# Window attention, forward and backward, on one core: P and dS of five quads turned on TensorE, and the first loads in another order

## The chip, the cores and the metric

The kernel runs on one core of a Trainium2 chip. The core has TensorE (PE in the profile: matrix products; PEld is its loading of weights), VectorE (DVE), ScalarE (ACT), GpSimd (POOL) and SyncE (SP). SyncE, ScalarE and GpSimd issue transfers (DMA) here; each issues its own in the order of its instructions, and an instruction that waits holds up what stands behind it on the same engine. The metric is the device time of one execution in microseconds (us). Before the change it is 1906.21, the median of three runs (1904.59 to 1907.18).

## The reference

An image `x` of 256 x 256 pixels with 384 channels is cut into 1024 windows of 8 x 8 pixels. In each window the 64 pixels attend to each other with one head, and the result goes through `wo`. The kernel returns this output and the gradients with respect to `x`, `wqkv` and `wo` for a given `grad_out`, all in bfloat16.

```python
qkv = xw @ wqkv                                   # xw: [1024, 64, 384]
q, k, v = qkv[..., :C], qkv[..., C:2 * C], qkv[..., 2 * C:]
p = softmax(einsum('bqc,bkc->bqk', q, k) * C ** -0.5)
o = einsum('bqk,bkc->bqc', p, v) @ wo
# and the vector-Jacobian product of this with grad_out: dx, dwqkv, dwo
```

## The kernel before

**Folded weights.** The kernel never forms q, k and v. It folds the weights into two 384 x 384 matrices: A from Q and K with the scale, B from V and `wo`. For that it needs the three column blocks of `wqkv` and `wo` in SBUF, turns each block on TensorE (`turn_blocks`, line 99) and multiplies them (`weight_product`, line 109). B turned is `BT_sb`, A turned is `AT_sb`.

**Quads.** The work goes in 128 quads. A quad has eight windows, held as four tiles (t = 0 to 3) of 128 partitions, each tile being two windows of 64 pixels; `LO` and `HI` are the two halves. For a quad the kernel loads `xq` (x) and `dq` (the gradient), needs both turned (`xT`, `dT`, channels on the partitions), and makes from them `yz` (the projections of x by A and of the gradient by B). From `yz` and `xT` come the scores and the raw gradient of P together (`sd`), from these the softmax P and its gradient dS (`ps`, both in one tile), and from P, dS and their transposes (`PS`) the outputs: `o` (output rows), `d` (gradient rows of x), and `Uq`, `Wq`, which go into the weight gradients.

**Three quads in flight.** `step(c, b, a, ahead)` (line 373) is one step of the loop. It does the scores, softmax and `uq`/`vq` products of quad b = i, the projections of quad a = i + 1, the attention of quad c = i - 1, and issues the loads of quad `ahead` = i + 4. From step 4 on it also does weight-gradient products of finished groups of three quads (`gf_rows`, `gf_halves`; tiles `pg`, `ph`). TensorE's order within a step is: scores `sd`, eight products `pj` for `uq` and `vq`, projection of the gradient (kind 0), projection of x (kind 1), `gf_rows`, then the attention's tiles `pw`, `pu`, `po`, `pd`, with `gf_halves` between them. The order of every engine is the order in which the program is written (`manual_schedule`). The products go to eight PSUM banks that are used in turn (`ring`), so a product waits until the tile eight places before it has been copied out.

**What waits for what around the change.**

- `soft` (line 203) is the softmax in six parts on VectorE, with one exponential on ScalarE. Part 0 begins with the maximum of the scores, `mx` (line 208); the text uses its start as the mark of a step. Part 5 makes dS.
- The transposes of P and dS are made in two ways. For most quads `turn` (line 258) does it on VectorE, with one transpose of 32 x 32 blocks and four moves (lines 267 and 271). For the quads with `crossed` (0 to 3 and the last, line 420) it is a DMA: `stack` (line 242) copies P into the tile `cr` on ScalarE, part 5 of `soft` writes dS into it with two more subtractions on VectorE (line 239), and SyncE issues a DMA transpose `PS<-cr` (line 264). `cr` has one buffer.
- SyncE's queue takes, in each iteration: `load_turn` of quad i + 2 (DMA transposes `dT<-dq` and `xT<-xq`, line 151), `to_tokens` of quad i (the DMA transpose `tok<-zy`, line 188), `PS<-cr` in the five crossed quads, and the four loads of `xq` of quad i + 4 (line 144). Quad 3 is loaded at the start of iteration 0 and quad 4 in step 0.
- `gather` (line 180) copies `yz` to `zy` on VectorE in two parts, the second in the middle of the attention; `zy` has two buffers, so it waits for the `tok` transfer of two quads before. `tok` is used by the attention one step later.
- GpSimd's queue takes the four `dq` loads of a quad (line 142) and the outputs `o` and `d` (lines 316 to 325).

**The start.** `fetch_weights` (line 75) loads V's columns of `wqkv` and `wo`, each split over SyncE and ScalarE. `load_first` (line 128) loads the gradient of quad 0 over both in turn, then Q's columns on SyncE and K's on ScalarE (`fetch_rest`), then x of quad 0 on SyncE; a copy on GpSimd holds that engine until the last gradient tile has landed. TensorE does seven products on zeros (`warm_up`), turns V, makes `BT_sb`, turns the gradient of quad 0, turns Q, projects, turns K and x of quad 0, makes A, turns the gradient of quad 1 and projects again. `wo` itself is turned after step 1 (line 499). **The end** runs `gf_final` and `weight_gradients`.

Of the kernel before, what the change touches and what calls it, by code (L numbers as in the profile page):

```python
# [9 lines left out]
ALU = mybir.AluOpType  # L10
# [4 lines left out]
P = 128  # L15
# [8 lines left out]
def kernel(  # L24
# [50 lines left out]
    def fetch_weights():  # L75
        wo_in = wo.rearrange("(m p) n -> p m n", p=P)
        nc.sync.dma_start(out=w_sb[:, 0:2, columns(2)], in_=w_in[:, 0:2, columns(2)])
        nc.scalar.dma_start(out=w_sb[:, 2, columns(2)], in_=w_in[:, 2, columns(2)])
        nc.scalar.dma_start(out=wo_sb[:, 0:2, :], in_=wo_in[:, 0:2, :])
        nc.sync.dma_start(out=wo_sb[:, 2, :], in_=wo_in[:, 2, :])  # L80

    def fetch_rest():
        nc.sync.dma_start(out=w_sb[:, :, columns(0)], in_=w_in[:, :, columns(0)])
        nc.scalar.dma_start(out=w_sb[:, :, columns(1)], in_=w_in[:, :, columns(1)])
# [14 lines left out]
    def turn_blocks(dst, src, first=0):  # L99
        for k in range(CK):  # L100
# [3 lines left out]
            copy_out(k, dst[:, k, :], pt[:])  # L104

    def weight_product(dst, left, right, sc):
        for mr in range(CK):
# [4 lines left out]
            if sc is not None:  # L112
                nc.scalar.activation(out=dst[:, mr, :], in_=pc[:], func=ACT.Copy, scale=sc)
            else:
                copy_out(mr, dst[:, mr, :], pc[:])
# [12 lines left out]
    def load_first(st):  # L128
        st["xq"] = xq = grp.tile([P, QUAD, C], BF16, tag="xq", name="xq", bufs=2 * GQ + 5)
        st["dq"] = dq = qp.tile([P, QUAD, C], BF16, tag="dq", name="dq", bufs=6)  # L130
        for t in range(QUAD):
            (nc.sync, nc.scalar)[t % 2].dma_start(out=dq[:, t, :], in_=windows(grad_out, st, 2 * t))
        fetch_rest()
        for t in range(QUAD):
            nc.sync.dma_start(out=xq[:, t, :], in_=windows(x, st, 2 * t))
        nc.gpsimd.tensor_copy(out=spare[:, 0:1], in_=dq[:, QUAD - 1, 0:1])

    def load(st):
# [4 lines left out]
        for t in range(QUAD):  # L143
            nc.sync.dma_start(out=xq[:, t, :], in_=windows(x, st, 2 * t))
# [58 lines left out]
    def soft(st, step):  # L203
# [29 lines left out]
        else:  # L233
            pd = sm.tile([P, QUAD, WT], F32, tag="pd")
            nc.vector.tensor_tensor(out=pd[:], in0=st["Pb"], in1=over_k(st["D"][:]), op=ALU.mult)
            if st["crossed"]:
                cr = st["cr"]
                for w, h, o in ((0, LO, HI), (1, HI, LO)):
                    nc.vector.tensor_tensor(out=cr[o, :, w, :], in0=st["pr"][h, :, :], in1=pd[h, :, :], op=ALU.subtract)
            nc.vector.tensor_tensor(out=st["dS"], in0=st["pr"][:], in1=pd[:], op=ALU.subtract)  # L240

    def stack(st):
        if st["crossed"]:
            st["cr"] = cr = qp.tile([P, QUAD, 2, WT], BF16, tag="cr", name="cr", bufs=1)
            for w, h in ((0, LO), (1, HI)):
                nc.scalar.copy(out=cr[h, :, w, :], in_=st["Pb"][h, :, :])
# [11 lines left out]
    def turn(st):  # L258
        ps = st["ps"]
        st["PS"] = dst = qp.tile([P, 2, QUAD, WT], BF16, tag="PS", name="PS")  # L260
        if st["crossed"]:
# [111 lines left out]
    def step(c, b, a, ahead):  # L373
# [31 lines left out]
        for rows in range(1 if a is not None else 2):  # L405
            if fill:
                gf_rows(*fill.pop(0))
# [133 lines left out]
```

## Time and profile before

| What | Before |
|---|---|
| median of three runs | 1906.21 us (1904.59 to 1907.18) |
| profiled execution, its own time | 1906.89 us |
| its span | 1905.1 us |
| TensorE busy | 1892.1 us (99%) |
| VectorE busy | 1667.7 us (88%) |
| ScalarE busy | 1526.8 us (80%) |
| share of TensorE in the chain that ended last | 96% |
| `sd`: mean of one, 128x64 | 193 ns |
| `tok<-zy`, issue to landing, median | 7.8 us |
| `PS<-cr`, issue to landing, least / median / most | 2.5 / 4.8 / 7.1 us |

The page of a profile gives the busy time of each engine, the chain of work that ended last (followed back from the last instruction, at each step to what released it), and groups of equal instructions. Other views answer questions on a stretch of time: the timeline (start, duration, engine, line, operation, and in brackets how long the engine was idle before and what released it), the waits (who waited for what: total us, times, longest), the chain in order of time (start, duration, what), and windows (busy time of each engine, the clock granted to TensorE as PEclk, the busy share of the DMA engines and GB/s in each stretch). "SPq" and "ACTq" are the sequencers of SyncE and ScalarE; the duration of a DMA there is that of its issue, not of the transfer. TensorE's matmuls are pipelined, so their durations overlap; the distance between starts tells more.

### The profile page before, as it was taken

To read this page: it belongs to the slowest core of one execution; us is meant where nothing else is said; L and a number is where in the kernel's file an instruction comes from. 1 tells how busy PE (TensorE), PEld (TensorE's weight loads), DVE (VectorE), ACT (ScalarE), POOL (GpSimd) and SP (SyncE) were. 2 spreads that over 40 slices of the span, in tenths; PEclk is the share of its full clock that TensorE was granted. 3 is DMA by queue.
4 is the path that set the end of the run, shared out by engine and by line. 5 is a ranking of instruction groups with operands and counts; after the bars stand their busy time and mean duration, and the time that the engine had idled before them with its cause. 6 is when DMAs were issued, how large, how long until landed. Compare 5 with 4: busy or idle time off the path is not lost.

```text
span 1905.1 us, 57100 instructions
## 1 busy us (share of the span) xinstructions
PE 1892.1 (99%) x22333; PEld 1127.1 (59%) x22333; DVE 1667.7 (88%) x3613; ACT 1526.8 (80%) x3355; POOL 861.8 (45%) x1572
## 2 busy tenths in 40 slices
PE   9999999999999999999999999999999999999999
PEld 5565655655665566556555655665566556556655
DVE  5888888888888888888888888888888888888887
ACT  7877887888788888878887888788788878887884
POOL 4444444444454445444444544444445445444432
PEclk9999999999999999999999999999999999999999
DMA  9999999999999999999999999999999999999994
GB/s 208 218 226 204 219 222 230 217 217 216 223 220 214 222 216 219 218 210 228 216 217 206 228 217 223 217 219 214 220 221 219 217 212 222 223 216 221 195 202 104
DMA packets 949647, 408.34 MB, mean 214 GB/s; under 512 B 831232, under 2 KB 924864, under 8 KB 949376
## 3 DMA queue, kind: packets, MB, share of 16 engines
q1 hardware_dynamic: 873056, 253.08, 77.6%
q0 software_dynamic: 75072, 150.72, 31.4%
q8 instruction: 175, 2.87, 0.6%
q10 hardware_dynamic: 1248, 0.89, 0.2%
q14 instruction: 96, 0.79, 0.1%
HBM read 101.84 MB, written 101.84 MB: 107 GB/s over the span
## 4 chain that ended last, share of the span: by engine, by line
PE 96%; DMA 2%; ACT 1%; DVE 1%; issue 0%; DVEq 0%; ACTq 0%
PE pj L162 51%; PE pg L162 13%; PE ph L351 13%; PE sd L162 5%; PE pw L296 5%; PE pu L296 4%; PE po L296 4%; DMA tok<-zy 1%; PE pd L296 1%; DMA w_sb<-in_wqkv_dram 0%; DMA PS<-cr 0%; PE pe L429 0%; ACT yz L176 0%; ACT yz L178 0%; PE pt L103 0%
## 5 line engine op out<-in xcount | busy, mean ns | idle before, releaser
L316 POOL DMA_DIRECT2D out_dram<-o x512 | 274.5, 536 | 897.3 <-ACT o L300 885.3
L307 ACT CAST Wq<-pw 128x384 bf16<-128x384 f32 x506 | 244.0, 482 | 280.4 <-PE pw L296 280.3
L162 PEld LDWEIGHTS <-xT 128*128 128x128 bf16 x3072 | 291.7, 98 | 182.5 <-issue 0.5
L162 PE MATMUL pj<-B_sb,xT 128*128 128x384 bf16 x1536 | 333.4, 326 | 0.1
L162 PE MATMUL pj<-AT_sb,xT 128*128 128x384 bf16 x1536 | 333.3, 326 | 0.0
L142 POOL DMA_DIRECT2D dq<-in_grad_out_dram x508 | 268.8, 537 | 96.1 <-DMA out_dram<-d 38.3
L310 DVE CAST Uq<-pu 128x384 bf16<-128x384 f32 x512 | 283.1, 553 | 13.2 <-PE pu L296 1.1
L318 POOL DMA_DIRECT2D out_dram<-d x480 | 279.3, 582 | 15.4 <-ACT uq L256 6.8
L162 PE MATMUL pj<-dT,BT_sb 128*128 128x512 bf16 x1152 | 269.5, 379 | 0.0
L162 PE MATMUL pj<-xT,A_sb 128*128 128x512 bf16 x1152 | 269.5, 379 | 0.0
L296 PE MATMUL pd<-tok,ps 64*64 64x384 bf16 x2048 | 257.3, 327 | 1.9 <-DMA tok<-zy 1.5
L176 ACT CAST yz<-pj 128x512 bf16<-128x512 f32 x384 | 224.0, 587 | 36.7 <-PE pj L162 28.4
L300 ACT CAST o<-po 128x384 bf16<-128x384 f32 x512 | 249.8, 488 | 1.5 <-PE po L296 1.1
L256 ACT CAST vq<-pj 128x384 bf16<-128x384 f32 x512 | 247.0, 482 | 3.2
L256 ACT CAST uq<-pj 128x384 bf16<-128x384 f32 x512 | 244.3, 477 | 4.4 <-PE pj L162 2.5
L178 ACT CAST yz<-pj 128x512 bf16<-128x512 f32 x384 | 224.5, 588 | 22.8
L271 DVE STREAM_TRANSPOSE PS<-ps 32x256 bf16<-32x256 bf16 x492 | 214.5, 436 | 9.4
L162 PEld LDWEIGHTS <-xq 128*128 128x128 bf16 x1572 | 153.6, 98 | 115.3 <-issue 0.9
L351 PEld LDWEIGHTS <-xq 64*64 64x64 bf16 x6000 | 176.2, 107 | 67.7
L351 PE MATMUL ph<-Wq,xq 64*64 64x384 bf16 x3984 | 204.5, 322 | 0.0
L162 PEld LDWEIGHTS <-A_sb 128*128 128x128 bf16 x1152 | 112.7, 98 | 135.7
L162 PEld LDWEIGHTS <-BT_sb 128*128 128x128 bf16 x1152 | 112.7, 98 | 122.1
(93 smaller groups left out, 3060.0 us busy)
## 6 DMA issues: line engine op xcount, KB each, us to landing
xq<-in_x_dram SPq DMA_DIRECT2D x512, 96.0 KB, 4.0
out_dram<-o POOLq DMA_DIRECT2D x512, 96.0 KB, 4.0
dq<-in_grad_out_dram POOLq DMA_DIRECT2D x508, 96.0 KB, 5.9
out_dram<-d POOLq DMA_DIRECT2D x480, 96.0 KB, 4.6
out_dram<-d POOLq DMA_DIRECT2D x64, 48.0 KB, 5.1
tok<-zy SPq DMA_TRANSPOSE x128, 7.8
xT<-xq SPq DMA_TRANSPOSE x127, 7.2
dT<-dq SPq DMA_TRANSPOSE x126, 7.9
```

The lines of the kernel that those rows point to most:

```text
L142: nc.gpsimd.dma_start(out=dq[:, t, :], in_=windows(grad_out, st, 2 * t))
L162: nc.tensor.matmul(out, lhsT=lhsT, rhs=rhs, start=start, stop=stop)
L176: ENG[EV["z"][mo]](out=yz[:, mo, :, 0:4:3, :], in_=pj[:])
L178: ENG[EV["y"][mo]](out=yz[:, mo, :, 1:3, :], in_=pj[:])
L256: cp(out=dst[:, t, :], in_=pj[:])
L296: nc.tensor.matmul(dst[o, :], lhsT=operand(st, lhs, t, h), rhs=operand(st, rhs, t, h), **flags)
L300: copies[EV[name][i]](out=sb[rows, :], in_=src[rows, :])
L307: copies[EV["W"][t] if st["i"] >= GQ else "DA"[t % 2]](out=st["Wq"][:, t, :], in_=pw[:])
L310: copies[EV["U"][t]](out=st["Uq"][:, t, :], in_=pu[:])
L316: nc.gpsimd.dma_start(out=windows(out_0, st, 2 * t), in_=o)
L318: nc.gpsimd.dma_start(out=windows(out_1, st, 2 * t - 1), in_=d if t else above[:])
L351: nc.tensor.matmul(dst[o, :], lhsT=st["xq"][h, t, ma * P + o.start:ma * P + o.stop], rhs=st["UW"[f] + "q"][h, t, :], start=(i == 0), stop= ...
```

## The change

Three things are changed together.

1. **The turn of P and dS** in quads 0 to 3 and the last. `stack`, `cr` and the DMA transpose are gone. `turn` instead makes sixteen small products with the identity on TensorE into one PSUM tile, and one copy on ScalarE brings it to `PS`. It now stands on TensorE between the products of `gf_rows` (or the projection of x) and the attention; the VectorE form for the other quads stays where it was. `operand` loses its case for the crossed layout.
2. **The first loads.** ScalarE issues V's columns, `wo` and Q's columns, each as one transfer. SyncE issues the four gradient loads of quad 0, then K's columns, then x. GpSimd's holding copy now waits for the first x tile of quad 0. A one-column copy on ScalarE stands ahead of its first real copy. TensorE turns the gradient of quad 0 before it makes `BT_sb`. The copies of A are shared between ScalarE and VectorE.
3. **x of the fourth to sixth quads** (3, 4 and 5 counted from 0). Quads 3 and 4 are loaded in the start, ahead of the DMA transposes of quad 2; step 0 loads nothing. x of quad 5 is issued by GpSimd behind its gradient.

`wo` is now turned within step 1, between the two projections, with all copies on VectorE.

```diff
     def fetch_weights():
...
+        nc.scalar.dma_start(out=w_sb[:, :, columns(2)], in_=w_in[:, :, columns(2)])
+        nc.scalar.dma_start(out=wo_sb[:], in_=wo.rearrange("(m p) n -> p m n", p=P))
+        nc.scalar.dma_start(out=w_sb[:, :, columns(0)], in_=w_in[:, :, columns(0)])
...
     def weight_product(dst, left, right, sc):
...
-            if sc is not None:
+            if sc is not None and mr % 2:
                 nc.scalar.activation(out=dst[:, mr, :], in_=pc[:], func=ACT.Copy, scale=sc)
+            elif sc is not None:
+                nc.vector.tensor_scalar(out=dst[:, mr, :], in0=pc[:], scalar1=sc, scalar2=None, op0=ALU.mult)
...
     def load_first(st):
...
-            (nc.sync, nc.scalar)[t % 2].dma_start(out=dq[:, t, :], in_=windows(grad_out, st, 2 * t))
-        fetch_rest()
+            nc.sync.dma_start(out=dq[:, t, :], in_=windows(grad_out, st, 2 * t))
+        nc.sync.dma_start(out=w_sb[:, :, columns(1)], in_=w_in[:, :, columns(1)])
...
-        nc.gpsimd.tensor_copy(out=spare[:, 0:1], in_=dq[:, QUAD - 1, 0:1])
+        nc.gpsimd.tensor_copy(out=spare[:], in_=xq[:, 0, 0:1])
...
     def load(st):
...
-            nc.sync.dma_start(out=xq[:, t, :], in_=windows(x, st, 2 * t))
+            (nc.gpsimd if st["i"] == AHEAD + 1 else nc.sync).dma_start(out=xq[:, t, :], in_=windows(x, st, 2 * t))
...
-            if st["crossed"]:
-                cr = st["cr"]
-                for w, h, o in ((0, LO, HI), (1, HI, LO)):
-                    nc.vector.tensor_tensor(out=cr[o, :, w, :], in0=st["pr"][h, :, :], in1=pd[h, :, :], op=ALU.subtract)
...
-    def stack(st):
-        if st["crossed"]:
-            st["cr"] = cr = qp.tile([P, QUAD, 2, WT], BF16, tag="cr", name="cr", bufs=1)
-            for w, h in ((0, LO), (1, HI)):
-                nc.scalar.copy(out=cr[h, :, w, :], in_=st["Pb"][h, :, :])
...
     def turn(st):
...
-        if st["crossed"]:
...
-            nc.sync.dma_start_transpose(out=whole.rearrange("p t s k -> p t (s k)"),
-                                        in_=st["cr"][:].rearrange("p t w k -> p (t w k)"))
+        if st["on_pe"]:
+            pt = ring.tile([P, 2, QUAD, WT], F32, tag="r", name="pt")
+            for s in range(2):
+                for t in range(QUAD):
+                    for h in (LO, HI):
+                        nc.tensor.matmul(pt[h, s, t, :], lhsT=ps[h, s, t, :], rhs=ident[h, h], start=True, stop=True)
+            nc.scalar.copy(out=dst[:], in_=pt[:])
             return
...
     def step(c, b, a, ahead):
...
-        B(turn)
+        if b is not None and not b["on_pe"]:
+            turn(b)
+        if b is not None and b["i"] == 1:
+            turn_blocks(woT_sb, wo_sb, act=False)
...
+        if b is not None and b["on_pe"]:
+            turn(b)
         slots = attention(c) if c is not None else iter(())
...
         warm_up(7)
+        nc.scalar.copy(out=spare[:], in_=B_sb[:, 0, 0:1])
...
         load_turn(sts[1])
+        load(sts[3])
+        load(sts[4])
         turn_blocks(wT[2], w_sb, 2 * CK)
+        turn_on_pe(sts[0], "dq", "dT")
         weight_product(BT_sb, wo_sb, wT[2], None)
-        turn_on_pe(sts[0], "dq", "dT")
...
-            if i == 0:
-                load(sts[AHEAD - 1])
-            step(get(i - 1), get(i), get(i + 1), get(i + AHEAD))
-            if i == 1:
-                turn_blocks(woT_sb, wo_sb)
+            step(get(i - 1), get(i), get(i + 1), get(i + AHEAD) if i else None)
```

## The prediction

> **What bounds the kernel now.** I read the page first: the engines' busy time, then the chain that ended last.
>
> ```profile
> span 1905.1 us, 57100 instructions
> PE 1892.1 (99%) x22333; PEld 1127.1 (59%) x22333; DVE 1667.7 (88%) x3613; ACT 1526.8 (80%) x3355; POOL 861.8 (45%) x1572
> ...
> PE 96%; DMA 2%; ACT 1%; DVE 1%; issue 0%; DVEq 0%; ACTq 0%
> ```
>
> TensorE holds 96% of the chain. The timeline gives the pace: the first max of a quad's scores (`mx`) starts 14.56 us after that of the quad before, again and again from quad 12 to the end. No part of the change touches that loop, so all that can move lies before 192 us and after 1866 us. There the starts of `mx` are 19.96, 29.01, 43.34, 59.64, 72.12, 87.00, 102.03, 116.64, then every 14.56 to 174.90, and 191.80. In steps 0 to 3 no weight-gradient products are due yet, so these could be shorter than 14.56; steps 1 and 2 take 14.33 and 16.30 all the same. Step 5 (15.03) and step 11 (16.89) are over the pace by 0.47 and 2.33.
>
> The chain of waits between 40 and 56 us and the SyncE queue name the cause in step 2:
>
> ```profile
> 44.31 6.87 DMA PS<-cr
> 51.18 0.02 issue
> 51.20 0.04 ACTq L246
> ```
>
> ```profile
> 39.25 4.96 SPq L188 DMA_TRANSPOSE tok<-zy  x1
> 44.31 3.20 SPq L264 DMA_TRANSPOSE PS<-cr  x1
> 47.57 2.88 SPq L144 DMA_DIRECT2D xq<-in_x_dram  x4
> ```
>
> The turned P and dS of quad 1 stand in SyncE's queue behind `tok`. They land at 51.18, and only then may `cr`, which has one buffer, be written for quad 2. ScalarE's queue stops at that copy, and the projections' copies stand behind it. The waits of ScalarE, VectorE and TensorE in the first 200 us (a line each, from their three answers):
>
> ```profile
> ACT cr L246 <- DMA PS<-cr: 4.4, 1, 4.4
> ```
>
> ```profile
> DVE cr L239 <- DMA PS<-cr: 2.2, 1, 2.2
> DVE zy L184 <- DMA tok<-zy: 4.4, 3, 2.8
> ```
>
> ```profile
> PE pw L296 <- ACT uq L256: 1.6, 1, 1.6
> PE pd L296 <- DMA tok<-zy: 1.5, 1, 1.5
> ```
>
> The last of these is step 11: `tok` of quad 10 landed at 185.88. From the landings, `tok` came before its use by 6.5, 2.9, 6.2, 3.8, 0.0, 0.5, 1.7, 3.2, 4.5 and 1.3 us for quads 0 to 9, was late for quad 10, and is 9 to 12 us early from quad 21 on. So the transfers begin with little lead, nearly lose it, and win it back later.
>
> Step 3 is the measure of an early step without a stall, from VectorE's timeline:
>
> ```profile
> 59.64 0.88 DVE L208 TENSOR_REDUCE mx<-sd 64x4 f32<-64x256 f32 x2
> ...
> 67.56 0.56 DVE L307 CAST Wq<-pw 128x384 bf16<-128x384 f32 x1 [0.25 <-PE pw L296]
> ...
> 72.12 0.88 DVE L208 TENSOR_REDUCE mx<-sd 64x4 f32<-64x256 f32 x2
> ```
>
> TensorE is busy without a gap to 67.15, VectorE takes over at 67.56, and its copies run back to back for 4.56 us to the next `mx`. That chain makes 12.48 us. Anything put on TensorE ahead of the attention lengthens it.
>
> **The change, part by part.**
>
> *Turns on TensorE, steps 0 to 3 and the last quad.* Added to each: 16 products of 64x64 by 64 columns, and one ScalarE copy of 128x512 (0.59 us by the row of `yz`). The nearest row in columns is `sd`, 24 products of 64 columns in 0.81 us of the chain, 0.034 each: 16 take 0.54, and I take 0.5. Below, the attention has 12 products of 384 columns in 0.49, four at a time; two at a time with 64 columns that is 0.014 each, 0.2 a quad. Above, nine 128x128 turns take 0.50, so 0.9. Removed: two copies to `cr` on ScalarE (0.82), two subtractions on VectorE (0.85), the DMA turn and the wait for it. The new wait is of TensorE for dS; VectorE has it in step 3 at 66.6 less the 0.85, before TensorE asks at 67.2. Behind that wait stands the whole attention. ScalarE's copy lies ahead of the copies of `o`, in the time of the `cr` copies taken away.
>
> - Step 0: the first scores of quad 1 waited for ScalarE's copies at 27.18, 27.66 and 28.15, and those stood behind `cr`. With 0.82 less there, TensorE fills the rest with its turn: quad 1 about 0.55 earlier (0 to 0.9).
> - Step 1: ScalarE idled 1.82 ahead of `cr`, its projection copies came late, and `Wq` began at 38.24, 9.46 after the last score. Now TensorE's own work ends that wait: step 3's 7.9 plus 0.55 for the turned `wo`, which moves from the step's end to its middle, plus 0.5, so `Wq` starts at 9.35. The three VectorE copies of `wo` (1.1) then lie in its idle time (1.49 at 37.65) and no longer ahead of `mx`, where two stood at 42.69. With 4.56 behind it the step is 13.65: 0.7 less (0.2 to 1.5).
> - Step 2: as step 3 with the turn, 12.48 + 0.5 = 13.0 for 16.30: 3.3 less (2.9 to 3.6). The half clock at 55 us goes with it.
> - Step 3: 0.5 more (0.2 to 0.9). Last quad: the attention at 1874 follows TensorE's products at once, so 0.5 more; its landed `PS` was not waited for.
>
> *First loads.* All of V's columns, `wo` and Q now go on ScalarE's queue, the four gradient loads and K on SyncE's. By the issue times and times to landing, before: V 3.8, `wo` 4.9, gradients 7.8, K 8.5, Q 9.7 us. The two queues then ran evenly (V's parts landed at 3.3 and 3.8, `wo`'s at 4.7 and 4.9). Sharing the same bytes evenly gives V 4.2, gradients 5.5, `wo` 6.9, K 7.3, Q 8.8. TensorE waited for Q to 9.79; now the late `wo` holds the first weight product to 6.9 and Q arrives about 1.0 earlier. Against it: the last two x loads of quad 0 reuse semaphores and wait for Q and a gradient, so they land near 12.0, about when TensorE wants them; GpSimd's gradient loads start at x's first landing, some 0.4 later than 7.73; and the first product may run on the half clock (below). ScalarE's table load (1.28 at 3.75) moves under the transfers; it delayed one copy by 0.3. I take 0, with 1.0 gained and 1.5 lost as bounds.
>
> *x early.* x of quads 3 and 4 (eight loads of 0.60 issue each) now stand in SyncE's queue ahead of the turns of quad 2 and of `tok` of quad 0, and x of quad 5 goes behind the gradients on GpSimd's (four at 0.54). In the old trace the DMA engines were full to 29 us and half idle after:
>
> ```profile
> 28.00:30.00 2.00, 1.84 (x30) 1.40 (x31) 1.49 (x4) 0.60 (x3) 0.00 (x0) 1.00 1.15 252
> 30.00:32.00 2.00, 2.00 (x14) 1.22 (x13) 0.85 (x3) 1.96 (x5) 0.00 (x0) 1.00 0.42 100
> 32.00:34.00 2.00, 2.00 (x12) 0.97 (x10) 1.85 (x6) 0.63 (x2) 0.00 (x0) 1.00 0.64 156
> 34.00:36.00 2.00, 2.00 (x11) 0.93 (x10) 1.89 (x5) 1.52 (x4) 0.00 (x0) 1.00 0.52 125
> ```
>
> (Last columns: granted clock, DMA share, GB/s.) Twelve loads of 98 kB at 250 to 350 GB/s are 3.4 to 4.7 us, so `tok` of quad 0 lands near 34.5 instead of 30.24. Its covers: VectorE's `zy` copy of step 1 waits for it (due about 35.5) and then TensorE (36.7). Cost 0, at worst 1.5. In return the turns of quad 3 follow at once, `tok` of quad 1 lands near 42 instead of 49.80, ahead of the outputs, and that of quad 2 near 51 instead of 60.92. Four DMA turns, 2.5 us to landing at the least, are gone as well. With 8 us or more of lead at quad 3 the stalls of steps 5, 6 and 11 should not come: 0.47 + 0.05 + 2.33 = 2.85 less (0 to 2.85).
>
> **Sum.** 0 - 0.55 - 0.7 - 3.3 + 0.5 - 2.85 + 0.5 = -6.4. The profiled execution took 1906.89 (span 1905.1 and 1.8 around it): 1900.5. It lies 0.7 above the median 1906.21 of the runs shown, so 1899.8. A measurement here tells 0.2%, 3.8 us, from no change.
>
> **The clock.** PEclk is 0.52 from 54.8 to 58.3 and 1.00 before and after, following a stretch (51.4 to 54.8) in which TensorE had 1.64 busy of 3.40. At the start the 512-column products come 0.43 apart against 0.215 later, and the first weight product's 384 columns 0.32 against 0.16, so this TensorE ran at half rate to about 7 us. If the half rate lasts one such stretch longer, the first weight product runs to 9.8 instead of 8.5 and Q's turn starts near 10.1: 1.5 us. The Trainium skill, "TensorE: Matmul & The Clock Gate", Part 4 (PE-mode transpose), speaks against this change here: it says that transposes don't count as busy for the gate in the same way, and after the change transposes of V and the gradients fill the stretch in which the old kernel had its first weight product. By that rule the sum would be 1901.3; no run here shows it yet.
>
> **Rivals.**
>
> 1. *The transfers stay the bound of steps 4 to 11.* TensorE arrives 4 us earlier at quad 4, and if `tok` does not keep ahead, the stalls of 5 and 11 return. For it: DMA full from 37 us on, and `tok` only just in time nine times. Against: 3 us of idle transfer time is filled and four turns go. Time 1899.8 + 2.85 = 1902.7.
> 2. *The start is slower.* The half clock above, or V, `wo` and Q at their late bounds, or `tok` of quad 0 late: 1.5, so 1901.3; two of them, 1902.8.
> 3. *Slower: the turns don't overlap on TensorE.* If each product took its whole 0.193 us (mean of a `sd` product), a quad's turns cost 3.1, and five of them 15.4 instead of 2.5: 1912.7. It would be no gain from (6.4 + 2.5) / 80 = 0.11 us each. Against: `sd`'s 24 come 0.034 apart, and the 64x64 products of the attention overlap.
> 4. *The change doesn't do what it says*, since the queue, not the turn, held step 2: `tok` and x stand there as before. Then only step 2's wait goes in part, some 2 us: 1904.2. Against: the wait of 4.4 names `PS<-cr`.
>
> **How the numbers follow.** Forecast 0.52; rival 1 0.17; rival 2 0.15; rival 3 0.07; rival 4 0.05; 0.04 for a larger stall in the start (slower). Faster by over 0.2% means under 1902.4: the forecast, most of 2 and a little of 1, 0.70. Within 0.2%: the rest of 1, 2 and 4, 0.19. Slower 0.11. Range: with the good bounds (1.0, 0.35, 0.8, 0.3, 0.3, 0.3) the sum is 3 lower, 1896.5, less 0.7 for runs; rivals 1 and 2 together reach 1904.2, with the same allowance 1905.
>
> **What would show it.** In the trace after: `mx` of quads 1 to 4 at about 28.5, 42, 55 and 68; no `cr`; the 16 turns of a quad within 0.5 us; Q's turn between 8.8 and 10; no wait for `tok` in steps 4 to 11, and `tok` of quad 3 landing 8 us or more before its use. I am wrong if step 3 is longer than 13.4, if TensorE waits for `xT` of quad 1 or `tok` of quad 0, or if the pace after quad 12 is not 14.56.

## The result and the profile after

The changed kernel takes 1901.89 us (median of 22 runs, 1900.64 to 1905.51), the kernel before 1905.72 in the 22 runs beside them (1903.20 to 1911.72). The ratio is 0.9977 with a 95% interval of 0.9971 to 0.9984: faster by 0.23%, some 4 us. The interval lies clear of no change, but its near end, 0.16%, is under the 0.2% that the prediction took as the least that a measurement tells. The profiled execution of the changed kernel took 1900.77, with a span of 1899.0 against 1905.1.

The first part of the page of the changed kernel, and its chain that ended last:

```profile
span 1899.0 us, 57224 instructions
PE 1889.7 (100%) x22413; PEld 1127.3 (59%) x22413; DVE 1664.4 (88%) x3606; ACT 1526.1 (80%) x3348; POOL 862.7 (45%) x1576
...
PE 99%; DVE 1%; DMA 0%; SPq 0%; issue 0%; ACT 0%
```

TensorE now holds 99% of the chain where it held 96%, and the transfers' 2% are gone. All waits of TensorE in the first 200 us of the changed kernel (who <- for whom: total us, times, longest):

```profile
PE pt L154 <- DMA dq<-in_grad_out_dram: 2.1, 3, 1.1
PE po L284 <- DVE Wq L295: 1.2, 3, 0.4
PE warm L85 <- DVE B_sb L82: 1.2, 1, 1.2
PE pw L284 <- DVE Uq L298: 0.7, 3, 0.2
```

No wait for `tok` is left. The first line is new, and stands in the start: TensorE waits three times for the gradient of quad 0. The marks of the steps, from VectorE's timeline:

```profile
21.33 0.88 DVE L204 TENSOR_REDUCE mx<-sd 64x4 f32<-64x256 f32 x2
30.07 0.88 DVE L204 TENSOR_REDUCE mx<-sd 64x4 f32<-64x256 f32 x2 [0.32 <-PE sd L158]
43.48 0.88 DVE L204 TENSOR_REDUCE mx<-sd 64x4 f32<-64x256 f32 x2
56.21 0.88 DVE L204 TENSOR_REDUCE mx<-sd 64x4 f32<-64x256 f32 x2
68.94 0.88 DVE L204 TENSOR_REDUCE mx<-sd 64x4 f32<-64x256 f32 x2
```

Steps 1 to 3 are 13.41, 12.73 and 12.73 instead of 14.33, 16.30 and 12.48; step 0 begins 1.37 us later. From step 5 on every step is 14.56 or 14.57. SyncE's queue in the stretch that was shown of before:

```profile
38.33 4.14 SPq L184 DMA_TRANSPOSE tok<-zy  x1
42.69 4.46 SPq L147 DMA_TRANSPOSE dT<-dq  x1
47.21 2.94 SPq L147 DMA_TRANSPOSE xT<-xq  x1
50.26 4.48 SPq L184 DMA_TRANSPOSE tok<-zy  x1
54.78 3.44 SPq L140 DMA_DIRECT2D xq<-in_x_dram  x4
```

The turn of quad 1 and the x loads of quad 5 no longer stand between two `tok` transfers: that of quad 2 is issued at 50.26 instead of 54.14.

The difference of the two profiled executions, part by part, beside the sum of the prediction (us, after less before):

| Part | Predicted | Measured |
|---|---|---|
| start to the first `mx` | 0 | +1.37 |
| step 0 | -0.55 | -0.30 |
| step 1 | -0.7 | -0.92 |
| step 2 | -3.3 | -3.57 |
| step 3 | +0.5 | +0.25 |
| stalls, steps 4 to 11 | -2.85 | -2.84 |
| last quad (step 123 -0.23, end +0.15) | +0.5 | -0.08 |
| sum | -6.4 | -6.1 |

### The profile page after: what moved, and what is told of

The parts are those of the page before. It is cut to its first block, busy times and chain, and to the rows that moved or that the text cites. A ratio compares the mean times of both kernels' runs of the same rounds, so it can differ in the third digit from the quotient of the medians.

```text
span 1899.0 us, 57224 instructions
## 1 busy us (share of the span) xinstructions
PE 1889.7 (100%) x22413; PEld 1127.3 (59%) x22413; DVE 1664.4 (88%) x3606; ACT 1526.1 (80%) x3348; POOL 862.7 (45%) x1576
## 4 chain that ended last, share of the span: by engine, by line
PE 99%; DVE 1%; DMA 0%; SPq 0%; issue 0%; ACT 0%
PE pj L158 52%; PE pg L158 13%; PE ph L339 13%; PE sd L158 5%; PE pw L284 5%; PE po L284 4%; PE pu L284 4%; PE pd L284 1%; PE pe L421 0%; DMA dq<-in_grad_out_dram 0%; PE pc L104 0%; PE pt L97 0%; DVE Uq L298 0%; DVE Wq L295 0%; DVE d L288 0%; SPq L128 0%
```

## The experiments

What they have to tell apart: whether the DMA turn itself made step 2 long or SyncE's queue did; which part keeps the transfers ahead of TensorE; and what made the start later. The three parts can be put in singly and in pairs. Unless said otherwise each is set against the kernel before in the same batch. A step is the distance between two starts of `mx`; "over the pace" is what all steps from 4 on have above the steps of the changed kernel.

### Part 1 alone: P and dS turned by TensorE

```diff
 before, and:
-        B(stack)
-        B(turn)
+        if b is not None and not b["on_pe"]:
+            turn(b)
...
+        if b is not None and b["on_pe"]:
+            turn(b)
         slots = attention(c) if c is not None else iter(())
```

> The kernel before with one part of the change: P and dS of quads 0 to 3 and of the last are turned by TensorE, at the place where the changed kernel does it (the turn of wo stays after step 1). First loads and x as before. Theory A (the wait of ScalarE's copy to cr for the DMA turn of quad 1 made step 2 long, and the lead of the transfers comes from x being early): steps 0 to 3 and the last quad change as between the two traces, -0.3, -0.6 to -0.9, -3.6, +0.25, about 0 at the end, and the stalls of steps 5 and 11 stay or grow, because TensorE comes 4 us earlier to the same transfers: time against before -0.5 to -4.5, with single steps from 4 to 12 over 14.6. Theory B (the four DMA turns taken off the queue give the lead by themselves): no stall in steps 4 to 11, -7 against before, 1.4 less than the changed kernel. Theory C (rival 4, the queue and not the turn held step 2): step 2 stays over 15, -2 at most.

Measured: 1902.27 (10 runs, 1901.24 to 1910.82) against 1905.62, ratio 0.9991 (0.9978 to 1.0003): by this interval not told from no change. In its trace, of one of the quicker runs (1901.49), the first `mx` is at 19.80, steps 0 to 3 are 8.74, 13.43, 12.83 and 12.73, and step 6 is 16.57. TensorE waits for `tok` once:

```profile
PE pd L288 <- DMA tok<-zy: 1.2, 1, 1.2
```

Theory C (rival 4) falls: with the DMA turn gone and the queue else as it was, step 2 is 12.83. Theory A holds: four steps are as in the changed kernel (step 1 too, 13.43 for 13.41, though `wo` is still turned after it here), and the transfers have no lead. `tok` came 0.8, 0.5 and 1.5 us before its use for quads 2 to 4 and 1.5 too late for quad 5.

### Part 3 alone: x of quads 3 to 5 early

```diff
 before, and:
-            nc.sync.dma_start(out=xq[:, t, :], in_=windows(x, st, 2 * t))
+            (nc.gpsimd if st["i"] == AHEAD + 1 else nc.sync).dma_start(out=xq[:, t, :], in_=windows(x, st, 2 * t))
...
+        load(sts[3])
+        load(sts[4])
         turn_blocks(wT[2], w_sb, 2 * CK)
...
-            if i == 0:
-                load(sts[AHEAD - 1])
-            step(get(i - 1), get(i), get(i + 1), get(i + AHEAD))
+            step(get(i - 1), get(i), get(i + 1), get(i + AHEAD) if i else None)
```

> The kernel before with x of quads 3 to 5 loaded early and nothing else: P and dS are still turned by DMA, the first loads are as before. Theory A (the wait for PS<-cr is the cause in step 2): x now stands ahead of the first turns, tok of quad 0 lands later than 30.24 us and the turn of quad 1 about when it did (51.2) or a few us earlier; step 2 stays over 14.5 and step 1 over 14; the stalls of steps 5 and 11 (2.85 together) go in part or whole: 0 to -4 against before. Theory C (x in the queue held the turn): step 2 falls to 13 and the time by 4 to 6. If early x only delays the first turns, the time is 0 to +3.

Measured: 1903.89 (12 runs), ratio 0.9987 (0.9978 to 0.9997). The profiled execution, the longest of the twelve (1909.05), has step 1 at 16.83 and step 2 at 12.65: their sum is 29.48, against 30.63 before and 26.14 after. ScalarE and TensorE wait in its first 200 us:

```profile
ACT cr L246 <- DMA PS<-cr: 4.3, 1, 4.3
```

```profile
PE pd L296 <- DMA tok<-zy: 3.8, 3, 1.8
```

The wait for `PS<-cr` is as long as before (4.4), but a step earlier: now `tok` of quad 0 comes late (35.05), the turn of quad 0 behind it lands at 35.77, and the `cr` of quad 1 waits for that. So no single step is a measure of this wait; where it falls depends on the queue, and it is gone in every trace without the DMA turn. The sign that was set for step 2 failed: at 12.65 it is what theory C gave, not the 14.5 or more of theory A. What speaks for A is the wait itself, the sum of both steps, and the time, which fell by 1.7 and not by 4 to 6. Steps 4 to 12 are 7.0 us over the pace, more than the 2.85 before, where theory A had these stalls go in part or whole. Early x gave this execution no lasting lead.

### Part 2 alone: the first loads

```diff
 before, and:
+        nc.scalar.dma_start(out=w_sb[:, :, columns(2)], in_=w_in[:, :, columns(2)])
+        nc.scalar.dma_start(out=wo_sb[:], in_=wo.rearrange("(m p) n -> p m n", p=P))
+        nc.scalar.dma_start(out=w_sb[:, :, columns(0)], in_=w_in[:, :, columns(0)])
...
+        nc.gpsimd.tensor_copy(out=spare[:], in_=xq[:, 0, 0:1])
...
+        turn_on_pe(sts[0], "dq", "dT")
         weight_product(BT_sb, wo_sb, wT[2], None)
-        turn_on_pe(sts[0], "dq", "dT")
```

> The kernel before with the new first loads alone (V, wo, Q on ScalarE; gradients and K on SyncE; the gradient of quad 0 turned ahead of the first weight product; GpSimd's gate on x). Theory A (the gradient's turn placed ahead of the weight product costs the start): first max of quad 0 at 21.3 instead of 20.0 us, and the half clock from 7.8 to 11.2; of the 1.4 the stalls on transfers of steps 2, 5 and 11 may swallow some: 0 to +1.5 against before. Theory D (the first loads gain, and the lateness in the changed kernel comes from its other parts): first max at 20.0 or earlier, 0 to -1.

Measured: 1906.93 (12 runs), ratio 1.0010 (1.0002 to 1.0019): slower, by 0.1%. First `mx` at 20.47, between the 21.3 of theory A and the 20.0 of theory D, and later than in all six traces of kernels with the old first loads (18.53 to 19.96). That is theory A in its direction, and without a half clock at that place. Steps 1 and 2 are 16.85 and 17.34; nothing after step 3 is over the pace until step 123 (0.7). TensorE comes some 4 us later to quad 4 than before (76.73 for 72.12), which may be why.

### All but part 2

```diff
 the changed kernel, with fetch_weights, fetch_rest, load_first, the copies of A,
 the order of BT_sb and the gradient's turn as before, without the one-column copy
```

> The changed kernel with the first loads of the kernel before (turns on TensorE and early x stay). Theory A (the new first loads only cost): first max of quad 0 at 19.0 to 19.8 us instead of 21.3, steps 0 to 3 as in the changed kernel (8.75, 13.4, 12.73, 12.73), no stall in steps 4 to 11: span 1896.6 to 1897.5, a median of 1900.0 to 1900.5. Theory F (the landing of tok of quad 0, not TensorE, sets step 1 once x stands ahead of it, and the lead of the transfers in the changed kernel comes from its later start): tok of quad 0 lands later than 36 us, step 1 is over 14.5 or stalls of 1 to 3 us come back in steps 4 to 12, and the median is 1902 or more.

Measured: 1899.21, 1899.04 to 1899.76 in five runs, against 1906.93 for the kernel before in that batch; ratio 0.9959 (0.9947 to 0.9972). Its slowest run is below the quickest of the 23 of the changed kernel (1900.37, below), and its median is the lowest of the study, though one kernel below (1899.62) isn't told apart from it. First `mx` at 19.37, then 8.75, 13.40, 12.73, 12.73, and nothing over the pace. Its TensorE waits in the first 200 us for no `tok` and no gradient:

```profile
PE po L288 <- DVE Wq L299: 1.2, 3, 0.4
PE warm L91 <- DVE B_sb L88: 1.2, 1, 1.2
PE pt L103 <- DMA w_sb<-in_wqkv_dram: 0.7, 1, 0.7
PE pw L288 <- DVE Uq L302: 0.7, 3, 0.2
```

Theory A holds: the new start as it stands, loads, order and gate, only costs. The median is 0.8 below the 1900.0 to 1900.5 of that theory. `tok` of quad 0 had 0.70 us to spare, so theory F was near.

### All but part 3

```diff
 the changed kernel, with:
-            (nc.gpsimd if st["i"] == AHEAD + 1 else nc.sync).dma_start(out=xq[:, t, :], in_=windows(x, st, 2 * t))
+            nc.sync.dma_start(out=xq[:, t, :], in_=windows(x, st, 2 * t))
...
-        load(sts[3])
-        load(sts[4])
...
-            step(get(i - 1), get(i), get(i + 1), get(i + AHEAD) if i else None)
+            if i == 0:
+                load(sts[AHEAD - 1])
+            step(get(i - 1), get(i), get(i + 1), get(i + AHEAD))
```

> The changed kernel with x of quads 3 to 5 loaded where the kernel before loads it. Theory A (early x gives the lead of the transfers): tok of quad 0 lands near 31 us with 6 us to spare, but from quad 2 on tok comes less than 3 us ahead of its use and 2 to 3 us of stalls stand in steps 4 to 12, as in the kernel with the turns alone: median 1903 to 1905. Theory F (the lead comes from the four DMA turns that are gone and from the later start): no stall, median within 1 us of the changed kernel, 1901 to 1902.5.

Measured: 1906.09 (11 runs, 1900.66 to 1911.27) against 1906.93, ratio 0.9996 (0.9983 to 1.0008): without early x the other two parts gain nothing on the median. Its trace, of the longest of the eleven (1911.27), has step 2 at 18.91 and 5.2 us over the pace after it: 1.5 in step 4 and 3.7 in steps 98 to 100. SyncE's queue and TensorE's wait:

```profile
31.64 5.93 SPq L140 DMA_DIRECT2D xq<-in_x_dram  x8
37.82 1.61 SPq L147 DMA_TRANSPOSE dT<-dq  x1
39.54 2.72 SPq L147 DMA_TRANSPOSE xT<-xq  x1
42.31 8.23 SPq L184 DMA_TRANSPOSE tok<-zy  x1
```

```profile
PE pd L284 <- DMA tok<-zy: 5.2, 2, 4.5
```

Eight x loads stand between `tok` of quad 0 and the transposes of the next, `tok` of quad 1 is issued at 42.31 instead of 38.33, right as the outputs of that step go out, and lands at 55.57 instead of 47.33. Theory A holds: without early x the lead is gone. The places were forecast wrong: `tok` of quad 0 landed at 35.06 and not near 31, most of the loss stands in step 2, and the median is 1 us over the range.

Measured medians, from several batches, with the ratio to the kernel before of the same batch; the ratios are what can be compared:

| | x as before | x early |
|---|---|---|
| old first loads, DMA turns | 1905.6 | 1903.9 (0.9987) |
| old first loads, turns on TensorE | 1902.3 (0.9991) | 1899.2 (0.9959) |
| new first loads, DMA turns | 1906.9 (1.0010) | not run |
| new first loads, turns on TensorE | 1906.1 (0.9996) | 1901.9 (0.9977), the change |

Turns and early x give 0.09% and 0.13% alone and 0.41% together. The intervals are wide enough that a plain sum isn't excluded; that the two parts need each other rests on the traces, with their 2.0, 7.0 and 5.2 us over the pace where one is missing and none where both are there as in the change.

### The first weight product ahead of the gradient's turn

```diff
 the changed kernel, with:
-        turn_on_pe(sts[0], "dq", "dT")
         weight_product(BT_sb, wo_sb, wT[2], None)
+        turn_on_pe(sts[0], "dq", "dT")
```

> The changed kernel with the first weight product put back ahead of the gradient's turn on TensorE, nothing else. Theory A (the turn that waits for the last gradient, 7.88 us, holds the weight product, whose wo lands at 5.2): the product starts at 5.3, the turn follows when the last gradient is in, Q's turn starts near 9.5 instead of 11.1 and the first max near 19.8 instead of 21.3: 1.5 less than the changed kernel, 5 to 7 less than before. Theory E (the half clock from 7.8 to 11.2 is set by what TensorE did earlier and comes in any order): Q's turn at 10.3 or later, less than 0.8 gained.

Measured: 1903.77 (11 runs), ratio 0.9994 (0.9984 to 1.0004): not faster than the changed kernel. Theory E falls, since the turn of Q moved to 8.45 and the first projection to 9.18, 2.5 earlier than in the changed kernel. Theory A holds that far and no further. The first `mx` came only to 20.73: the turn of quad 1's gradient took TensorE from 13.75 to 16.32 instead of 0.67, as its loads on GpSimd had begun at 10.47. And step 1 took 17.60:

```profile
25.60 4.21 SPq L147 DMA_TRANSPOSE xT<-xq  x1
29.92 8.75 SPq L184 DMA_TRANSPOSE tok<-zy  x1
```

```profile
PE pj L158 <- DMA xT<-xq: 2.4, 1, 2.4
```

`xT` of quad 2 landed at 38.14, 2.4 us after TensorE wanted it, and `tok` of quad 0 at 41.19 (36.78 in the changed kernel). What TensorE won in the start it lost to transfers that did not move with it.

### The same, with GpSimd's gate back on the gradient

```diff
 the kernel above, with:
-        nc.gpsimd.tensor_copy(out=spare[:], in_=xq[:, 0, 0:1])
+        nc.gpsimd.tensor_copy(out=spare[:], in_=dq[:, QUAD - 1, 0:1])
```

> The changed kernel with the first weight product ahead of the gradient's turn and GpSimd's gate back on the last gradient of quad 0; the new first loads stay. Theory G (two things cost the start of the changed kernel: the turn's place, and the gate on x that sends GpSimd's gradient loads off at 10 instead of 7 us, so that TensorE waits for quad 1's gradient when it comes earlier): no wait for quad 1's gradient between 13 and 17 us, the projections of quad 0 start near 9.2 and the first max of quad 0 at 18.7 to 19.2, 0.2 to 0.6 ahead of the kernel with the old first loads (19.37): median 1898.6 to 1899.2, if tok of quad 0 still lands in time. Theory H (the queue of first loads itself costs): first max at 20 or later, median 1900.5 or more.

Measured: 1899.62 (5 runs, 1898.19 to 1900.15), ratio 0.9965 (0.9952 to 0.9977). The first `mx` is at 18.29, the earliest of all: theory G. The median is above the 1898.6 to 1899.2 of that theory, and in the trace step 1 is 15.64, since the turned gradient of quad 2 landed at 32.92:

```profile
PE pj L158 <- DMA dT<-dq: 2.1, 1, 2.1
```

The loads alone, without order and gate, do bring Q earlier: it landed at 7.33 to 8.38 in the eight traces with the new loads, at 8.31 to 9.74 in the six with the old. The first projection starts at 8.63 here and at 8.96 in the last of the next two kernels, whose start is the same, against 8.87 to 10.30 with the old loads. Nothing of that reaches the end: the ratio isn't told apart from the 0.9959 (0.9947 to 0.9972) of the kernel with the old loads, and in the trace the transfers of step 1 bind.

### Fewer or later x loads

Two kernels tried to free those transfers.

```diff
 all but part 2, with x of quad 4 loaded in step 0:
         load(sts[3])
-        load(sts[4])
...
-            step(get(i - 1), get(i), get(i + 1), get(i + AHEAD) if i else None)
+            step(get(i - 1), get(i), get(i + 1), get(i + AHEAD))
```

> The changed kernel with the old first loads (as in the run before that took 1899.2), and x of quad 3 alone ahead of the first step; x of quad 4 goes on SyncE's queue in step 0, behind tok of quad 0, and x of quad 5 on GpSimd's as in the changed kernel. If the order on SyncE's queue is what tok waits for, tok of quad 0 lands 2 to 3 us earlier (33 to 34 us for 35.87), with 2.5 to 3.5 us to spare instead of 0.70. If four loads of x are lead enough, steps 4 to 12 stay at 14.56 and the median is 1899.0 to 1899.4; if the lead needs both quads' x, tok of quads 2 to 5 comes less than 2 us before its use and 1 to 3 us of stalls return: 1900.5 to 1903.

Measured: 1900.42 (8 runs, 1899.00 to 1903.64), ratio 0.9974 (0.9963 to 0.9984). The trace is of one of the two longest of the eight (1903.60). In it `tok` of quad 0 landed at 34.40 with 2.15 to spare, 1.5 us earlier where 2 to 3 were expected, but `tok` of quad 1 was 2.25 late, step 2 took 15.87 and step 3 14.03. Steps 4 to 12 are at the pace all the same. In this execution four loads were not lead enough for quad 1; the median lies between the two ranges, and the interval overlaps that of the kernel with both quads' x, so whether four loads cost on the median stays open.

```diff
 the kernel with the gate back, and:
-        load(sts[4])
...
                 load_turn(sts[i + 2])
+            if i == 0:
+                load(sts[AHEAD])
```

> The kernel of the run before (new first loads, weight product first, gate on the gradient) with x of quad 4 moved on SyncE's queue from ahead of quad 2's turned gradient to behind it and its turned x, still ahead of tok of quad 0. There TensorE waited 2.1 us for the turned gradient of quad 2, which landed at 32.92. If the order on the queue is what held it, it lands at 29.5 to 31, that wait goes, tok of quad 0 lands at 36 to 37.5 and TensorE, which wants it near 35.5, waits 0.5 to 2 us for it: step 1 at 13.9 to 15.4, median 1898.0 to 1899.5. If the bytes up to 37 us set the end of step 1 whatever their order, the first max of quad 2 stays at 42.5 to 43 and the median at 1899.3 to 1900.

Measured: 1902.69 (11 runs, 1898.89 to 1906.89), ratio 0.9983 (0.9973 to 0.9992). The turned gradient of quad 2 landed at 27.98 in place of 32.92, and `tok` of quad 0 at 38.40, 2.6 us late:

```profile
PE pd L284 <- DMA tok<-zy: 2.3, 1, 2.3
```

The first `mx` of quad 2 came at 43.67, not earlier than the 42.68 of the kernel above. The wait only changed its name: the second theory in kind, but the median is some 3 us worse than either expected. This trace starts with less lead and keeps less: `tok` came 2.0 to 4.5 us ahead for quads 1 to 9 and was just late for quad 10, and step 11 is 0.5 over the pace. Step 53 is over by 1.8 too, but not for this: `tok` was 9 us ahead there, and TensorE idled 1.7 us for a reason that the profile doesn't name.

### Both kernels once more, and the price of a turn

> The changed kernel once more, unchanged, for a second trace. If the half clock after 7.8 us belongs to the order of the work, it is there again and the first max is at 21.3; if it comes from how the gradient loads fall in a run, the first max is between 19.8 and 21.3. Steps 2 and 3 at 12.73 and the pace of 14.56 from quad 4 on should be the same to 0.1 us; what varies between runs should be in step 1, where tok of quad 0 had only 1.75 us to spare.

One run, 1900.37. No half clock after a full one this time (full rate began late instead, see below), first `mx` at 20.93, then 8.74, 13.41, 12.73, 12.73 and nothing over the pace. `tok` of quad 0 had 0.28 us to spare.

> The kernel before once more, unchanged, for a second trace. If the wait of ScalarE's copy to cr for the DMA turn is there in every execution, step 2 (quad 2 to quad 3) is over 15.5 again; the stalls on tok should stand in other steps than 5 and 11, between 1 and 6 us in all, since this kernel's times go from 1902.1 to 1912.5; the pace elsewhere 14.56.

One run, 1905.19. Step 2 took 15.34 and step 1 15.23 (sum 30.57, before 30.63), so the wait for `PS<-cr` is there again (ScalarE 5.5 us in two waits). Two larger stalls stand in steps 6 and 10 (15.40 and 16.51), 2.9 in all. I had expected more than 15.5 in step 2; the sum of steps 1 and 2 is what stays.

```diff
 the changed kernel, with:
-    sts = [{"at": q, "i": i, "on_pe": i <= GQ or i == n - 1} for i, q in enumerate(quads)]
+    sts = [{"at": q, "i": i, "on_pe": True} for i, q in enumerate(quads)]
```

> The changed kernel with P and dS turned by TensorE in all 128 quads instead of 5; VectorE's transpose and the copies behind it go from the other 123. It measures the price of a turn where TensorE is the bound: at 0.25 us a quad (step 3 of the changed kernel against before) the time grows by 31 us, at the 0.5 of the prediction by 61, at the 0.2 of its lower bound by 25, and at 3.1 (rival 3, no overlap) by 380. Less than 20 means that the other engines' relief pays for part of it.

One run, 1957.11, span 1955.3. The pace is 14.98 instead of 14.56, 0.42 a quad: between the 0.25 of step 3 and the 0.5 of the prediction. All 16 turns of a quad in the timeline of the changed kernel (step 3, the lines between them are other products that overlap):

```profile
63.72 0.38 PE L252 MATMUL pt<-ident,ps 64*64 64x64 bf16 x12
...
63.93 0.23 PE L252 MATMUL pt<-ident,ps 64*64 64x64 bf16 x4
63.99 0.33 PE L284 MATMUL pw<-dq,ps 64*64 64x384 bf16 x2
```

From the first turn to the first product of the attention that isn't mixed in with them are 0.27 us. Rival 3 falls: 0.42 / 16 = 0.026 a product, not 0.193. In this trace step 1 was 16.84: TensorE waited 2.4 us for `xT` of quad 2, which landed at 37.94, and 0.4 for `tok` of quad 0, which landed at 40.94. The start is that of the changed kernel, so its step 1 can fall into these waits too.

## What made the start later

In TensorE's timeline before, the first weight product and the turn of Q were:

```profile
5.13 2.65 PE L110 MATMUL pc<-wT,wo_sb 128*128 128x384 bf16 x9
9.79 0.68 PE L103 MATMUL pt<-ident,w_sb 128*128 128x128 bf16 x9 [1.34 <-DMA w_sb<-in_wqkv_dram]
```

TensorE's timeline in the start of the changed kernel (in brackets how long it was idle, and what ended that):

```profile
4.16 0.78 PE L97 MATMUL pt<-ident,w_sb 128*128 128x128 bf16 x9
4.78 0.33 PE L154 MATMUL pt<-ident,dq 128*128 128x128 bf16 x3
6.16 0.34 PE L154 MATMUL pt<-ident,dq 128*128 128x128 bf16 x3 [1.05 <-DMA dq<-in_grad_out_dram]
7.30 0.34 PE L154 MATMUL pt<-ident,dq 128*128 128x128 bf16 x3 [0.80 <-DMA dq<-in_grad_out_dram]
7.93 0.50 PE L154 MATMUL pt<-ident,dq 128*128 128x128 bf16 x3 [0.29 <-DMA dq<-in_grad_out_dram]
8.22 3.09 PE L104 MATMUL pc<-wT,wo_sb 128*128 128x384 bf16 x9
11.10 0.73 PE L97 MATMUL pt<-ident,w_sb 128*128 128x128 bf16 x9
```

`wo` was there at 5.21 and Q at 8.13. The product started at 8.22, because the turn that now stands ahead of it waits for the last gradient load, at 7.88. In the kernel with the order put back:

```profile
5.57 1.64 PE L104 MATMUL pc<-wT,wo_sb 128*128 128x384 bf16 x9 [0.51 <-DMA wo_sb<-in_wo_dram]
7.05 0.95 PE L154 MATMUL pt<-ident,dq 128*128 128x128 bf16 x9
```

The same product also takes 3.09 in one trace and 1.64 in the other. The windows of the changed kernel (length, busy us of PE, PEld, DVE, ACT, POOL, then PEclk, DMA share, GB/s):

```profile
4.39:7.81 3.42, 1.40 (x18) 0.88 (x16) 1.09 (x4) 0.96 (x2) 0.00 (x0) 1.00 1.07 291
7.81:11.22 3.41, 3.29 (x14) 1.78 (x15) 0.79 (x2) 0.96 (x2) 1.36 (x3) 0.50 0.75 190
```

After a stretch with 1.40 busy of 3.42 the clock is half for 3.41 us. By the distances between starts of products, full rate began at 4.4, was lost from 7.8 to 11.2, and returned. In the second trace of this kernel full rate did not begin before 10.5, and the product took 2.83. In three others with the same order (first loads alone; all but early x; all turns on TensorE) it began at 5.9 to 6.4 and was kept, and the product took 1.63 each. So, by these five traces, the half clock is not a property of the order: the order opens a gap, and when full rate begins in an execution goes with whether the gap costs more than its own length. The later start is no accident of two executions either: the first `mx` is at 20.01 to 21.33 in the five traces with this order, 20.64 on average, and at 18.53 to 19.96 in the six with the old first loads, 19.33 on average.

## Why the prediction was right or wrong

**The total.** Forecast 1899.8, measured 1901.89, inside the range of 1895.8 to 1905.0; the sign was right, by a small margin. The sum for the profiled execution, -6.4, came out as -6.1. That it fits to 0.3 is luck in part: the start was missed by 1.37, and the other terms together came out 1.1 better than forecast. By the written bounds the low end of the sum is 1896.75, not 1896.5. The medians differ by 3.8 only: the profiled execution of before lay 1.2 above the median of its 22 runs, that of after 1.1 below. The allowance of 0.7 for the first was too small, and none was made for the second. The runs of after reach to 1905.5. Two traces of it show 0.28 and 1.75 us to spare at `tok` of quad 0, and two kernels with the same loads (all turns on TensorE; the product put first) show what late transfers cost there, 3.4 and 4.2 us in step 1, where TensorE waits 2.4 us for `xT` of quad 2 as well. That this is what the runs above 1903 have is argued from it, not traced.

**Step 2, the mechanism: right.** The wait for `PS<-cr` was the cause; with the turns alone the step falls to 12.83. The size was 3.57 for 3.3. The trace of one execution misled in one thing: part of the wait can stand in step 1, where `before` in its second trace and early x alone have it.

**Steps 0, 1 and 3, and the last quad.** The terms -0.55 and -0.7 measured -0.30 and -0.92. As written, the terms of step 1 (7.9, 0.55 and 0.5) make 8.95 and not 9.35; the 0.41 from TensorE's first attention product to `Wq` (67.15 to 67.56) is left out of the text, as is some 0.25 that comes off again, from the last score to `mx`. The move of `wo` into the step brought nothing that can be seen: step 1 is 13.43 without it and 13.41 with it. The turn's price was mis-sized: 0.25 in step 3 and 0.15 at the end for 0.5, by the `sd` row; the row of the attention's 64-partition products, which gave the lower end, was nearer. In the steady loop, where TensorE is the bound, 0.42.

**The start: wrong.** The step that failed is "now the late `wo` holds the first weight product to 6.9". The estimate of landings shared the bytes evenly between the two queues: V 4.2, gradients 5.5, `wo` 6.9, K 7.3, Q 8.8. The trace has 3.99, 7.88, 5.21, 9.04 and 8.13. The four gradient loads on one queue came out last, and the gradient's turn had been put ahead of the product. The term of 0 was +1.37, near its bound of +1.5, and that bound had been set for the half clock. A half clock did come, but in the second trace, where full rate began late instead of being lost, the first `mx` is only 0.4 earlier, and in two kernels with the same order and full rate 0.85 (all turns on TensorE) and 1.32 (all but early x). Of the new loads the arrival of Q was forecast well (8.8, landed 8.13); the order threw it away, and Q's turn began at 11.10, not between 8.8 and 10. Second miss in the same step: GpSimd's gradient loads "some 0.4 later than 7.73" began at 10.04. The first tile of x, last on SyncE's queue, landed at 9.31, and 0.7 more passed to the first issue, 0.4 of it after the holding copy, for a reason that the profile doesn't name. In the changed kernel this cost nothing, since TensorE turned quad 1's gradient at 16.25 without a wait; with the weight product put first it became a wait of TensorE, until the gate went back.

**The stalls: right in the sum, and by a lead that was over-estimated.** Forecast for `tok` of quads 0, 1 and 2: 34.5, 42 and 51; measured 36.78, 47.33 and 57.17, with 1.75, 3.9 and 6.8 to spare, and 6.06 at quad 3 instead of 8 or more. It held because both causes were taken away together: turns alone leave 2 us of stalls in steps 4 to 12, early x alone 7, both none in five traces (the change twice, without part 2, and with the order put back, with either gate). Rival 1 did not occur in the changed kernel, but it is what the traces show when either part is missing.

**Rivals.** 2 came true in its size, by another mechanism than the clock in the first place. 3 and 4 fell, to the run with all turns on TensorE and to the turns alone. For rival 1 the prediction counts `tok` as only just in time nine times; by the landings that it lists, it had 0.5 us or less for quads 4, 5 and 10. The rule of the Trainium skill weighed there ("TensorE: Matmul & The Clock Gate", Part 4 (PE-mode transpose): transposes don't count as busy for the gate in the same way) stays open. For it: in the second trace of the changed kernel the stretch from 3.72 to 7.13 had 2.42 us of TensorE at work, all but the first 0.4 us transposes, and full rate was not granted after it. Against it: in the three other traces with this order a stretch of 3.41 us with 2.06 to 2.35 at work, all but its last 1.2 to 1.5 us transposes, kept full rate. Zero products in the gaps would tell; that was not tried.

## How the lead may feed itself

In SyncE's queue `tok` either goes ahead of the outputs that GpSimd issues in the same step, or beside them. For `tok` of quads 2 to 12 in 13 traces (all but that with all turns on TensorE), counting the output transfers that GpSimd issued from 4 us before `tok`'s issue to the end of it:

```
outputs issued beside it    transfers of tok    mean, issue to landing
0 to 2                      46                   7.4 us
3 to 5                      37                   8.3 us
6 to 9                      60                  10.8 us
```

A longer issue has a longer time in which to meet outputs, but that isn't what the table shows: counted to a fixed 3.6 us from the issue, the means are 7.7, 9.3 and 11.0 us. A late `tok` meets eight outputs, takes 3.4 us longer and holds SyncE's queue meanwhile (its issue takes 5.7 us with eight beside it and 4.7 with none), so the next one tends to be late too; an early one goes ahead of them. This would explain why, for quads 4 to 12, `tok` is 6 to 13 us early in the five traces named above that have no stall, and 0 to 6 us in the two of the kernel before, and why a few loads moved by a few us decide between them. It is read from the traces and not shown; no run moved the outputs alone.

Nor does a lead keep itself always. With x of quad 3 alone early, `tok` was 1.6 to 4 us ahead at quads 4 to 6 and won its lead without a stall there. In the kernel without early x it was 12.7 us ahead at quad 95 and 0.3 at quad 97, after one `tok` that took 15.75 us to land; what made that one slow stays open.

## What to carry over

A price read from one execution of a kernel whose transfers are nearly late holds for that execution: trace both kernels twice, and set steps that share a wait against each other as a sum. Where several loads start together, ask which one the first instruction in TensorE's order needs, since an instruction put ahead inherits the latest of its inputs for all behind it. And a part that may help another (early x and the turns) is to be priced with it and without it: by the medians one gave 1.7 us here, the other 3.4, both 7.7, with intervals that leave the difference in doubt, and part 2, the first loads, cost some 3 of that (ratio 0.9977 against 0.9959).

## What was not expected of the hardware

- Full rate of TensorE began at 4.4 to 7.2 us in 13 of the 14 traces, whatever the kernel, and at 10.5 in one; the first weight product took 1.6 to 2.8 us for that reason alone, with the same order. Half-clock stretches were 3.41 or 6.83 us. In the trace of before full rate began at 7.12 and the half stretch at 54.91, 14 x 3.41 later. This agrees with the Trainium skill, "TensorE: Matmul & The Clock Gate", Part 1 (The HAM clock gate (the "warmup" mystery)), which has a free-running window of 3413 ns that does not start with the kernel.
- The PEclk figure reads 1.00 in the first microseconds, where 512-column products start 0.43 us apart, half of the later rate: at the beginning of a trace the distance between products is to be trusted, not the figure.
- The issue of one `tok` transpose took SyncE between 3.6 and 9.7 us in the 14 traces; an estimate of a queue from the durations of another execution can be off by as much.
